# Shift and scale of the first norm: w_mod as the moving operand in four column groups, and identity products in PE's gaps before the first scores

## The chip, the cores and the metric

The kernel runs on one core of a Trainium2 chip. The metric is the device time of one execution in microseconds. The core has five engines with queues of their own: PE (matrix products), DVE (vector), ACT (activation functions), POOL (a second, slower vector engine) and SP (which here only issues DMAs). Engines wait for each other by semaphores; within an engine everything runs in program order.

## The reference

One transformer block on 2048 tokens of width 1024, modulated by a single vector `c`. 32 query heads of width 32 share one key and one value head.

```python
mod = (_silu(c) @ w_mod).reshape(c.shape[0], 6, 1, -1)
sa, ca, ga, sb, cb, gb = ...                 # six vectors of 1024
h = _layernorm(x) * (1 + ca) + sa            # the first norm's scale and shift
x = x + ga * A(h, wq, wk, wv, wo)            # attention: softmax over 2048 keys
h = _layernorm(x) * (1 + cb) + sb
x = x + gb * B(h, w1, w3, w2)                # silu(h w1) * (h w3), times w2; inner width 3584
```

Scale and shift of the first norm are not applied to `x`. The scale `1 + ca` is multiplied into the rows of `wk`, `wv` and `wq`, and the shift `sa` becomes a bias on k, q and v (`sa` times the unscaled weights). So nothing of k or q can be finished before both are known.

## The kernel before

**The graph and its planner.** `build` does not emit instructions in order. It calls `op`, which records a node: engine, a function that gives its instructions, an expected duration, what it reads and writes, a due value `vt`, and a mode for PE (`F` full array, `S` scores in four row groups, `A` four column groups of 32). `Placer.run` then places one node after another on the engine where it can start first by expected durations, and among nodes that can start at nearly the same time takes the one with the lowest `vt` plus an offset. The offsets and four or five parameters come from `PLAN`, one entry for every eight scores, each changing the one before. The program thus holds five fixed queues, with waits where a node needs another engine's result. Some nodes have alternatives (ACT or DVE for a norm or a copy out of PSUM). Almost every instruction is issued by the helper `play` (line 22), so in the profile nearly all carry that line, and tile names tell them apart.

**Banks.** PSUM has eight banks. Six hold scores, in three pairs that are used in turn. Two (6 and 7, `PB` in the profile) serve everything else in sessions (`Sess`): a session keeps its bank until all that reads it is done, and the next session's first product waits for that. The transposes of the first tiles use score banks instead, as no score is due yet.

**The start.** SP issues the tiles of `x` (two tiles per DMA), four 1 MB pieces of `w_mod` (two fields, each in two halves), and `wq` in two pieces. For each of the 16 tiles of 128 tokens, `lnt1` does two halves of statistics (DVE, `ST`), an aggregate (`MV`), three small POOL steps (`RS`, `NB`), the normalization into `XN` (`XNB` or `WO` in the profile, on ACT or DVE), eight transposes on PE against `IDENT`, and a copy into `HT` (ACT or DVE).

`mod_cols(fld)` computes a vector of 1024 as eight columns of 128: for each of eight chunks `c` of the inner width and eight column sets `k`, a product with the weights as stationary operand and one column of silu(c) as moving operand, 64 products in two nodes of 32. DVE then reads eight columns: `MODC[:, 1]` (1 + ca) for field 1, `SAB` (sa) for field 0. `scale0` scales the k and v weights (`WKS`, spread to `WKR`) and the first 256 columns of `wq` (`WQ0S`, in eight pieces on DVE or POOL). `k_bias` and `q_bias` give `KBI` and `QBI`, `k_proj` and `q_proj` fill `KT` and `QT`. All of these go through the two banks.

**The rest.** 512 score steps follow, in the order of `CYC`: the first 16 alternate between two column blocks of heads, since only those q columns are scaled early. A score step is eight products, followed on ACT by two exps into a ring `U` of ten steps. Around them the planner places what else PE has: q projections, value products (`U,V`), row sums (`PS,ONES`), the output projection, and for each of eight blocks of 256 tokens the second norm and the feed-forward part in 14 slabs and four quarters. DVE adds pairs of exps (`PS`), and frees the ring with them. `prods` gives some products two forms, `full` and `cols` (four 32-column products), chosen by the mode PE is in.

## Time and profile before

| | us |
|---|---|
| median of 3 runs | 1138.04 (1136.25 to 1138.82) |
| the profiled execution | 1137.71 |
| its span in the trace | 1135.9 |
| first score on PE | 32.69 |
| first exp on ACT | 33.74 |
| end of the last exp | 1036.25 |
| PE, ACT, DVE, POOL busy | 1108.3, 1021.3, 992.1, 41.3 |

Times in the trace count from the start of the span. In a row of the timeline, the first number is the start, the second the length, then engine, line, instruction, what is written from what, shape and count; a bracket gives idle time ahead of it and what ended that. In a table of stretches, each engine's busy time is followed by the number of its instructions. The rows that the argument uses stand in the prediction.

### The profile page before, as it was taken

What the parts mean: (1) busy time and instruction counts of PE and PEld (TensorE: products, weight loads), DVE (VectorE), ACT (ScalarE), POOL (GpSimd) and SP (SyncE); (2) the same over time, 40 slices, a digit from 0 to 9 for tenths busy, and PEclk for the clock granted to TensorE, in tenths of its full rate; (3) what the DMA queues carried; (4) which work ended last, traced back from release to release, by engine and by line L of the source; (5) the groups of instructions that cost most, each with busy time, mean ns of one, the idle gap of its engine ahead of it and who ended that gap; (6) DMA issues with size and microseconds to landing.
All of it is one profiled execution on the core that took longest, in us unless ns stands there. A gap on an engine that the chain in (4) does not pass through costs nothing.

```text
span 1135.9 us, 38650 instructions
## 1 busy us (share of the span) xinstructions
PE 1108.3 (98%) x17512; PEld 757.2 (67%) x17512; DVE 992.1 (87%) x1614; ACT 1021.3 (90%) x1158; POOL 41.3 (4%) x92
## 2 busy tenths in 40 slices
PE   6899999999999999999999999999999999999998
PEld 6644446666567766777567766777577756776887
DVE  7988999998999889998998899988998889987532
ACT  5999999999999999999999999999999999994110
POOL 5200000000000000000000000000000000000000
PEclk9999999999999999999999999999999999999999
DMA  9320397665486658865596577768597568777993
GB/s 345 106 76 5 128 263 191 175 193 140 114 258 195 174 131 216 235 193 152 128 283 194 149 198 190 219 195 222 130 274 202 150 159 218 207 201 197 246 242 92
DMA packets 381540, 209.72 MB, mean 185 GB/s; under 512 B 17600, under 2 KB 373184, under 8 KB 381376
## 3 DMA queue, kind: packets, MB, share of 16 engines
q1 hardware_dynamic: 380944, 207.11, 65.8%
q8 instruction: 138, 2.26, 0.8%
q14 instruction: 26, 0.21, 0.1%
q10 hardware_dynamic: 432, 0.13, 0.0%
HBM read 199.89 MB, written 4.19 MB: 180 GB/s over the span
## 4 chain that ended last, share of the span: by engine, by line
PE 61%; ACT 25%; DVE 11%; issue 1%; POOL 1%; DMA 0%; DVEq 0%
PE PB L22 44%; ACT U L22 24%; PE S L22 16%; DVE PS L22 4%; DVE ST L22 2%; ACT HT L22 1%; DVE QT L22 1%; POOL RS L22 1%; DVE X L22 1%; DVE HT L22 1%; DVE RB L22 1%; DVE XNB L22 0%; DMA X<-in_A_x_dram 0%; DVE MV L22 0%; DVE RC L22 0%
## 5 line engine op out<-in xcount | busy, mean ns | idle before, releaser
L22 ACT ACTIVATE U<-S 128x1024 bf16<-128x1024 f32 x1024 | 964.6, 1131 | 7.2 <-PE S L22 6.3
L22 DVE TENSOR_TENSOR PS<-U 128x2048 bf16<-128x2048 bf16 x256 | 307.3, 1217 | 9.4 <-ACT U L22 7.9
L22 DVE TENSOR_TENSOR PS<-PS 128x1024 bf16<-128x1024 bf16 (+1 forms) x420 | 282.5, 690 | 3.4
L22 PE MATMUL PB<-QT,W 128*128 128x256 bf16 (+1 forms) x2992 | 229.8, 273 | 1.2 <-DVE HT L22 1.0
L22 PE MATMUL S<-QT,KT 32*128 32x256 bf16 x4096 | 203.8, 273 | 8.0 <-ACT U L22 5.0
L22 PEld LDWEIGHTS PB<-QT,W 128*128 128x128 bf16 (+1 forms) x2992 | 172.3, 97 | 44.3 <-issue 26.5
L22 PE MATMUL PB<-W2S,HT 128*128 128x256 bf16 x1512 | 188.4, 273 | 0.0
L22 PEld LDWEIGHTS PB<-W2S,HT 128*128 128x128 bf16 x1512 | 137.8, 98 | 39.4 <-issue 21.3
L22 PEld LDWEIGHTS S<-QT,KT 32*128 32x128 bf16 x4096 | 60.7, 92 | 139.8 <-ACT U L22 130.1
L22 PE MATMUL PB<-U,V 128*32 128x256 bf16 x4096 | 127.4, 273 | 0.9 <-ACT U L22 0.5
L22 PE MATMUL PB<-QT,HT 128*32 128x256 bf16 (+1 forms) x1560 | 116.0, 273 | 1.5 <-DVE HT L22 1.1
L22 PEld LDWEIGHTS PB<-U,V 128*32 128x32 bf16 x4096 | 101.6, 96 | 21.2 <-issue 12.7
L22 PE MATMUL PB<-HT,W 128*32 128x512 bf16 (+3 forms) x896 | 101.2, 336 | 0.1
L22 PEld LDWEIGHTS PB<-QT,HT 128*32 128x32 bf16 (+1 forms) x1560 | 85.3, 97 | 23.5 <-issue 14.1
L22 ACT ACTIVATE HT<-PB 128x512 bf16<-128x512 f32 (+1 forms) x105 | 74.4, 708 | 12.3 <-PE PB L22 12.3
L22 DVE SCALAR_TENSOR_TENSOR HT<-HT,PB 128x512 bf16<-128x512 bf16 x101 | 69.0, 684 | 8.1 <-ACT HT L22 8.0
L22 PEld LDWEIGHTS PB<-HT,W 128*32 128x32 bf16 (+1 forms) x896 | 51.1, 98 | 33.4 <-issue 10.5
L22 DVE TENSOR_TENSOR HT<-HT,PB 128x512 bf16<-128x512 bf16 x99 | 67.4, 681 | 2.5 <-PE PB L22 1.6
L22 ACT ACTIVATE HT<-S 128x512 bf16<-128x512 f32 (+1 forms) x16 | 11.5, 730 | 54.6 <-PE S L22 54.6
L22 DVE STREAM_TRANSPOSE RB<-PB 128x256 f32<-128x256 f32 x63 | 28.0, 444 | 37.3 <-PE PB L22 36.8
L22 PE MATMUL PB<-WO,QT 128*128 128x512 bf16 (+1 forms) x248 | 56.0, 381 | 1.1 <-DVE RB L22 1.1
L22 POOL TENSOR_SCALAR RS<-MV 128x1 f32<-128x1 f32 x32 | 11.6, 362 | 1004.5 <-DVE MV L22 1003.4
(107 smaller groups left out, 669.5 us busy)
## 6 DMA issues: line engine op xcount, KB each, us to landing
W<-in_B_w_dram SPq DMA_DIRECT2D x150, 512.0 KB, 4.6
W2S<-in_B_w_dram SPq DMA_DIRECT2D x30, 1792.0 KB, 8.5
HT<-in_B_w_dram SPq DMA_DIRECT2D x74, 512.0 KB, 4.6
W2S<-in_w_mod_dram SPq DMA_DIRECT2D x8, 1024.0 KB, 5.7
X<-in_A_x_dram SPq DMA_DIRECT2D x8, 512.0 KB, 7.5
U<-in_w_mod_dram SPq DMA_DIRECT2D x4, 1024.0 KB, 12.1
out_dram<-X SPq DMA_DIRECT2D x7, 512.0 KB, 7.4
W2S<-in_A_x_dram SPq DMA_DIRECT2D x5, 512.0 KB, 9.4
```

The lines of the kernel that those rows point to most:

```text
L22: return getattr(e, call[0])(*call[1], **call[2])
```

## The change

- `mod_cols` turns the operands round. silu(c) of a chunk is spread over 32 columns (`SCR`, a new copy on DVE) and becomes the stationary operand; the weights become the moving operand, 256 columns at a time, in four column groups of the array at once (`tile_position=(0, 32 * g)`). A half is 16 products of 256 columns instead of 32 of one column. The result lies along the free axis, the same in 32 rows of each group, so DVE transposes it in 32 x 32 blocks into `MT` and takes every first column. The nodes are now of mode `A`.
- `keep_warm`, called before a node of mode `F` is placed on PE and before the first score: if the planner expects a gap of at least 0.2 us, it issues products of `IDENT` with itself into score bank 5, as many as the gap holds at 0.075 us each. 70 of them come out.
- The transposes of tile 5 no longer use bank 5 but one of the two shared banks.
- The planner's expected durations of the first transposes and projections are lower.
- `PLAN` is new up to about step 300. The order of all queues follows from it: on PE it differs up to there and is the same from score 288 on; on SP it is the same through the start. All eight pieces of `WQ0S` are on DVE now (five on DVE and three on POOL before); ACT has one KT copy and DVE one HT copy more in the first part.

```diff
-        static = tt < 6
+        static = tt < 5
...
-        op("pe", tr, 0.95 if tt < 4 else 0.6, reads=[("XN", slot), "IDENT"], writes=bk, ...)
+        op("pe", tr, 0.58, reads=[("XN", slot), "IDENT"], writes=bk, ...)
...
+    SCR = Uf[:, 8 * 2048:8 * 2048 + 256].rearrange("p (c r) -> p c r", r=32)
+    MT = Uf[:, 8 * 2048 + 256:8 * 2048 + 1280].bitcast(F32).rearrange("p (x k i) -> p x k i", x=2, i=32)
+    op("dve", lambda: [lambda e: e.tensor_copy(SCR[:], SCC[:, 3, :].unsqueeze(2).broadcast_to([P, NC, 32]))], 0.2, ...)
...
             op("pe", lambda b, h=h: [lambda e, c=c, k=k: e.matmul(
-                BANK[b][:, k:k + 1], WM0[:, c, fld * D:(fld + 1) * D].rearrange("p (q k) -> p k q", k=NC)[:, k, :],
-                SCC[:, 3, c:c + 1], start=(c == 0 and k == 0), stop=(c == NC - 1), skip_group_check=True)
-                for c in range(4 * h, 4 * h + 4) for k in range(NC)], 1.6, ..., mode="F", ...)
+                BANK[b][32 * g:32 * (g + 1), 0:256], SCR[:, c, :],
+                WM0[:, c, fld * D + 256 * g:fld * D + 256 * (g + 1)], start=(c == 0), stop=(c == NC - 1),
+                tile_position=(0, 32 * g), skip_group_check=True)
+                for c in range(4 * h, 4 * h + 4) for g in range(4)], 0.45, ..., mode="A", ...)
+        op("dve", lambda b: [lambda e: e.transpose(MT[:, fld], BANK[b][:, 0:256].rearrange("p (i k) -> p k i", k=NC))], ...)
         if fld:
-            ... e.tensor_scalar(MODC[:, 1, :], BANK[b][:, 0:NC], 1.0, None, ALU.add)
+            ... e.tensor_scalar(MODC[:, 1, :], MT[:, fld, :, 0], 1.0, None, ALU.add)
         else:
-            ... e.tensor_copy(SAB[:], BANK[b][:, 0:NC])
+            ... e.tensor_copy(SAB[:], MT[:, fld, :, 0])
...
+        if e == "pe" and self.warm and self.step == 0 and n.mode == "F":
+            self.keep_warm(start)
...
+    def keep_warm(self, start):
+        product, need = self.warm
+        gap = start - max(self.t["pe"], need.fin)
+        if not need.done or gap < 0.2:
+            return
+        ...
+        sem, count = self.sem, int((gap - 0.05) / 0.075)
+        ...
+            for _ in range(count):
+                play(eng, product(REC))
...
+    pl.warm = (lambda e: e.matmul(BANK[5][:, 0:P], IDENT[:], IDENT[:], start=True, stop=True), ident)
```

The entries of `PLAN` itself are left out.

More of the change, by code (lines that the diff above doesn't have):

```diff
@@ L802, in tr @@
                 IDENT[:]) for cc in range(NC)]
-        op("pe", tr, 0.95 if tt < 4 else 0.6, reads=[("XN", slot), "IDENT"], writes=bk, vt=vt, mode="F", sess=s, post=0.145)
+        op("pe", tr, 0.58, reads=[("XN", slot), "IDENT"], writes=bk, vt=vt, mode="F", sess=s, post=0.145)
         dst = HT[:, :, tt * P:(tt + 1) * P]
@@ L882, in k_proj @@
             BANK[b][:, 0:256], WKR[:, 1, cc].rearrange("p r f -> p (r f)"), HT[:, cc, ts], start=(cc == 0),
-            stop=(cc == NC - 1)) for cc in range(NC)], 1.7 if j == 0 else 0.9, reads=["WKR1"] + hk,
+            stop=(cc == NC - 1)) for cc in range(NC)], 0.9, reads=["WKR1"] + hk,
            writes=[("k", j)], vt=vt, mode="F", sess=s, post=0.145)
@@ L1267, in build @@
     k_proj(0, -1690)
-    q_proj(0, 1, 0, -1690, 2.0)
-    q_proj(0, 1, 1, -1689, 1.5)
+    q_proj(0, 1, 0, -1690)
+    q_proj(0, 1, 1, -1689)
     k_proj(1, -1680)
@@ L1305, in build @@
     G.alias([("U", s, i) for s in range(8) for i in range(2)], [("WM0", fl, h) for fl in range(2) for h in range(2)])
+    G.alias([("U", 8, i) for i in range(2)], ["SCR", ("MT", 0), ("MT", 1)])
     ht = [("HT", cc, tt) for cc in range(NC) for tt in range(NTT)]
```

360 lines of the change are left out of this document (172 added, 188 removed).

## The prediction

> **What bounds the kernel now.** I read the page first, then busy time by stretch, then the start instruction by instruction.
>
> ```profile
> PE 1108.3 (98%) x17512; PEld 757.2 (67%) x17512; DVE 992.1 (87%) x1614; ACT 1021.3 (90%) x1158; POOL 41.3 (4%) x92
> ```
>
> PE is busy 98%, which suggests that less PE work is less time. The stretches say where that holds. I cut them at the starts of scores 0, 10, 16, 32, 64, 128 and 288 of 512, and behind the last exp (columns: stretch, length, then busy us and instructions of PE, PEld, DVE, ACT, POOL; clock, DMA share, GB/s).
>
> ```profile
> 32.69:54.49 21.80, 19.95 (x379) 15.07 (x378) 21.08 (x44) 21.68 (x25) 5.24 (x13) 1.00 0.20 66
> 54.49:65.51 11.02, 10.71 (x188) 4.68 (x189) 10.62 (x13) 11.02 (x13) 0.00 (x0) 1.00 0.01 1
> 65.51:95.75 30.24, 30.22 (x414) 13.28 (x415) 25.98 (x41) 29.86 (x33) 0.00 (x0) 1.00 0.20 72
> 95.75:154.26 58.51, 57.75 (x1129) 28.88 (x1129) 53.42 (x91) 58.51 (x65) 0.00 (x0) 1.00 0.33 110
> 154.26:279.85 125.59, 119.49 (x1861) 77.93 (x1862) 117.20 (x190) 124.57 (x143) 1.60 (x4) 0.99 0.69 188
> 279.85:593.81 313.96, 310.99 (x5077) 209.94 (x5078) 290.38 (x466) 311.60 (x354) 7.33 (x12) 1.00 0.70 189
> 593.81:1036.30 442.49, 440.62 (x7302) 304.43 (x7302) 406.40 (x640) 438.56 (x500) 7.57 (x12) 1.00 0.71 192
> ```
>
> From the first score to 279.85 ACT idles about 1.5 us in all: the exps set the pace there, and PE's 98% is mostly company. Only in scores 16 to 32 is PE full (30.22 of 30.24) while ACT waits. From 279.85 on both are nearly full. So time can be won in three ways: exps that start earlier, less other work on ACT behind that start, and shorter ACT waits. The start itself, on PE and then on DVE:
>
> ```profile
> 20.69 1.06 PE L22 MATMUL PB<-IDENT,XNB 128*128 128x128 bf16 x8
> 21.55 2.06 PE L22 MATMUL PB<-SCC,U 128*128 128x1 bf16 x32
> ...
> 24.96 2.88 PE L22 MATMUL PB<-HT,WO 128*128 128x256 bf16 x16 [0.25 <-DVE KBI L22]
> ...
> 28.41 2.79 PE L22 MATMUL PB<-HT,WO 128*128 128x256 bf16 x24 [0.19 <-ACT KT L22]
> 32.07 0.69 PE L22 MATMUL PB<-IDENT,WO 128*128 128x128 bf16 x8 [0.86 <-DVE MV L22]
> 32.69 0.40 PE L22 MATMUL S<-QT,KT 32*128 32x256 bf16 x8
> ```
> ```profile
> 22.68 0.71 DVE L22 TENSOR_SCALAR WO<-W,MODC 128x256 bf16<-128x256 bf16 x2 [0.20 <-DMA W<-in_A_wq_dram]
> 23.65 0.17 DVE L22 CAST SAB<-PB 128x8 bf16<-128x8 f32 x1 [0.27 <-PE PB L22]
> ...
> 24.75 0.16 DVE L22 COPY KBI<-PB 128x1 f32<-128x1 f32 x1 [0.21 <-PE PB L22]
> ...
> 26.26 2.42 DVE L22 BATCH_NORM_STATS2 ST<-W2S 128x6 f32<-128x512 bf16 x4
> ...
> 31.45 0.47 DVE L22 TENSOR_SCALAR QT<-PB,QBI 128x256 bf16<-128x256 f32 x1
> ...
> 55.93 0.42 DVE L22 COPY WO<-PB 128x256 f32<-128x256 f32 x1 [0.28 <-PE PB L22]
> ```
>
> The transposes tell the array's speed: eight take 1.06 us at 20.69 and 0.69 at 32.07, so the array is slow until the k products. The first score waits for QT. QT waits for the DVE queue and the q products, those for two alternating banks, and the scaled q weights for `wq`, on which DVE waited at 22.68.
>
> **The change, part by part.**
>
> *The four `mod_cols` blocks.* 128 one-column products (2.06 us per 32) become 64 of 256 columns, four abreast. The trace has that form elsewhere:
>
> ```profile
> 54.82 1.29 PE L22 MATMUL PB<-U,V 128*32 128x256 bf16 x40
> ```
>
> 1.29/40 is 32 ns each, so a block of 16 takes 0.5 us, 1.0 at half speed. That takes 4 to 6 us off PE, all ahead of score 0. DVE gets for each field a transpose of 128x256 (nearest row: one half-sum copy of that size at 55.93, 0.42 us; its input is strided, so up to twice that) and a copy like SAB's (0.17). The last block starts when its weights land instead of behind transposes at 21.55: I put SAB at about 21.5, where it ended at 23.82. But SP's order is the same through the whole start, so `wq` lands at 22.7 as before, and of these 2.3 us only 0 to 1 reach what follows.
>
> *The scaling of the first q weights.* The program's order puts all eight pieces on DVE; before, POOL did three.
>
> ```profile
> L22 DVE TENSOR_SCALAR W<-W,MODC 128x1024 bf16<-128x1024 bf16 x8 | 3.8, 481 | 0.1
> L22 DVE COPY HT<-PB 128x1024 bf16<-128x1024 bf16 x5 | 3.3, 680 | 0.0
> ...
> L22 DVE TENSOR_SCALAR WO<-W,MODC 128x256 bf16<-128x256 bf16 x5 | 1.5, 351 | 0.2 <-DMA W<-in_A_wq_dram 0.2
> ```
>
> One piece costs between 0.12 (a quarter of 481 ns) and 0.35; I take 0.25, since what the 351 holds of POOL's company goes: 2.0 us, to 24.7. Next on DVE come one statistics half (0.61) and the KBI copy, done at 25.45. The k products wait for it, because it frees their bank. The Trainium skill, "SBUF — State Buffer", section "SBUF: two separate sides", says that VectorE in a two-port mode and GpSimd shut each other out for whole instructions. By that rule a piece is near 0.12 and KBI comes 1.0 us sooner; the 351 beside POOL agrees, but no row shows a piece alone.
>
> *From KBI to the first score.* k0 runs 25.5 to 26.4 (28.41 row: 24 in 2.79, eight in 0.93); ACT empties it (0.47) by 27.05. QBI stands behind two more halves on DVE, so k1 runs 26.9 to 27.8, q0 to 28.7, q1 to 29.6. DVE does four halves (2.42) behind QBI and empties q0 by 29.9. First score: 30.0 instead of 32.69. If k0 and k1 run as in the 24.96 row (eight in 1.44), q1 ends at 30.2 and the score comes at 30.3; with all four at half the fast speed, at 31.2.
>
> *The identity products.* There are 70, in gaps the planner foresees. At the slow transposes' 0.13 us they are 9 us, 46 of them ahead of the 1+ca block. They read IDENT and write a bank that transposes now leave alone; PE's own queue alone waits for them. If a gap is shorter than foreseen, the transposes behind come up to 1 us late, and the wait for `wq` covers that.
>
> *What the exps win.*
>
> ```profile
> 33.74 1.01 ACT L22 ACTIVATE U<-S 128x1024 bf16<-128x1024 f32 x1
> 34.64 1.02 ACT L22 ACTIVATE HT<-PB 128x1024 bf16<-128x1024 bf16 x1
> 35.78 1.24 ACT L22 ACTIVATE XNB<-W2S,NB,RS 128x1024 bf16<-128x1024 bf16 x1
> ...
> 87.11 91.87 ACT L22 ACTIVATE U<-S 128x1024 bf16<-128x1024 f32 x100 [0.35 <-PE S L22]
> ```
> ```profile
> 29.50 0.47 ACT L22 ACTIVATE KT<-PB,KBI 128x256 bf16<-128x256 f32 x1 [1.14 <-PE PB L22]
> ```
>
> A score at 30.0 puts the first exp at 30.6, 3.1 us earlier (an HT copy stood ahead of it before). But ACT's new order has two KT, two norms and two HT copies behind the first exp, about 4.9 us at the distances between these rows, where it had two HT copies and a norm, 3.0. That leaves 1.2. DVE limits it further. From 22.68 to the first half-sum copy at 55.93 it hardly rests (1.4 us). It now starts at the same landing with one HT copy, one norm (as a W piece, 0.48) and three q pieces more, one KT and the SAB cast less: 0.6 to 1.5 us more. The half sums free the exps' buffers and PE's banks. So term A, the lead at score 16, lies between -0.5 and 1.6. I take **0.7**.
>
> *Scores 16 to 32.* 32 exps at 0.919 us (91.87/100) are 29.4; the stretch took 30.24 because PE was full. In the new order it holds 1.3 us less PE work (32 U,V products at 32 ns, and a net two 512-column products). Term B: **0.8**, between 0 and 0.85.
>
> *Scores 64 to 288.* ACT idles 1.0 + 2.4 us in 154.26 to 593.81, the most this part can give. Counting the order, by score 160 about 5 us more PE work is done than before, by 288 exactly as much, and from there PE's order is the same to the end, so a lead at 288 is kept. PE gets lighter where it was level with ACT (scores 176 to 208 and 240 to 272, by 0.5 to 1.7 us per 16 scores) and heavier at 80 to 160 (0.8 to 2.2), where PE had 6.1 us idle in 154.26 to 279.85. Term C: **0.9**, between -1 and 2.0.
>
> The sum is 0.7 + 0.8 + 0.9 = 2.4. The profiled execution took 1137.71 (span 1135.9 and 1.8 around it), 0.3 below the median 1138.04 and within the runs. 1137.71 - 2.4 = **1135.3**.
>
> **The rivals.**
>
> *1. The clock falls back before the k products.* PE can slow itself by waiting: after the wait in the first row the second stretch was granted half the clock.
>
> ```profile
> 176.28 0.40 PE L22 MATMUL S<-QT,KT 32*128 32x256 bf16 x8 [1.44 <-ACT U L22]
> ```
> ```profile
> 178.00:180.00 2.00, 2.00 (x17) 0.91 (x15) 1.93 (x3) 1.52 (x3) 0.00 (x0) 0.50 0.08 25
> ```
>
> In the new start PE waits some 2 us for KBI, with only one-column products and a few identity products around. Half speed for k and q puts the score at 31.2, so term A at about -0.5: 1136.5. Against it: the wait is short and the array was fed just before. The Trainium skill, "TensorE: Matmul & The Clock Gate", section "Part 1: The HAM clock gate (the "warmup" mystery)", gives about 3.4 us of sustained activity to full speed and an idle window of that length back to half. By it this goes either way, as the window runs free; the 178 row agrees.
>
> *2. DVE holds the start.* Its queue from 22.68 is at least as long as before. If the half sums come no earlier than 55.93, A is 0 and, with PE's gaps only moved, C is 0 too: 1137.71 - 0.8 = 1136.9. For it: 21.08 of 21.80. Against it: ACT, not DVE, was never idle there.
>
> *3. Slower: PE becomes the bound at scores 80 to 176.* There the new order raises PE's sum to within 0.5 to 1.1 us of ACT's per 16 scores (31.8 against 32.3 at 96 to 112). The sum counts 0.11 us for a full product of 256 columns (28.41 row: 2.79/24), a quarter for one four abreast, and 0.1 for a change of array mode (32.69 row: 0.40 for eight four abreast, whose columns are 0.26). It decides from about 3% more than the sum; at 6% the six stretches lose about 7 us, of which PE's lighter work behind them gives back 2.4: 1142. Against it: in scores 16 to 32 such a sum gave 30.0 and the trace 30.24.
>
> *4. The blocks do not stream abreast.* Then a block takes 16 x 0.18 = 2.9 us (24.96 row) instead of 2.06, SAB comes near 24 and the score 1.5 later: A at -0.8, 1136.8. The 32 ns of the U,V row speak against it.
>
> **How the numbers follow.** 0.2% of 1138.04 is 2.3 us, about what a measurement of this kernel can tell from no change; faster by over that means under 1135.8. Forecast 0.56, rival 1 0.10, rival 2 0.17, rival 3 0.14, rival 4 0.03. Of the forecast's own range (A, B, C at their ends together give 1133.3 to 1138.2; ends rarely meet, so mostly 1133.3 to 1136.8) about 0.46 lies under 1135.8; a little of rivals 1 and 2 does too: faster 0.50. Rival 3 and the worst of the rest give slower 0.14; same 0.36. The range reaches from the forecast's low end past rivals 1, 2 and 4 to 1138.6 and leaves out rival 3.
>
> **What would show it.** Right: first score near 30.0, with `wq` still landing at 22.7; eight WQ0S pieces in about 2 us; score 16 some 0.7 and score 32 some 1.5 earlier; ACT's idle time from score 64 to 288 under 3.4 us; everything behind score 288 shifted by one amount. Wrong: k products of 1.4 us and more for eight (rival 1), half-sum copies at 56 with ACT waiting ahead of score 11 (rival 2), ACT waits for S at scores 80 to 176 (rival 3), blocks over 2 us (rival 4).

## The result and the profile after

The changed kernel takes 1143.27 us (median of five runs, 1141.81 to 1145.23) against 1137.81 (five runs, 1136.25 to 1138.82). The ratio is 1.0054, 95% interval [1.0038, 1.0071]: 5.5 us slower (4 to 8 by the interval), where 1135.3 had been forecast. The profiled execution is the one of 1143.27 us; its span is 1141.5.

The line of busy times on the page, and from PE's list of waits the line that the kernel before does not have (columns: total us, times, longest):

```profile
PE 1104.5 (97%) x17732; PEld 753.8 (66%) x17758; DVE 992.0 (87%) x1620; ACT 1020.9 (89%) x1158; POOL 41.4 (4%) x89
```
```profile
PE PB L22 <- issue: 5.8, 14, 1.9
```

Every engine works as long as before, within 4 us; what grew is idle time (PE's from 27.6 to 37.0 us). "issue" means that PE waited for nothing that the profile shows. Of its 14 times, three are waits, of 1.92, 1.73 and 0.36 us; the other eleven, of 0.16 us each, lie where the trace lacks the record of a product (it has 26 products less than weight loads). The stretches, cut at the same scores as before (0, 10, 16, 32, 64, 128, 288, end of the exps):

```profile
30.21:54.88 24.67, 21.45 (x385) 16.69 (x387) 22.62 (x51) 22.70 (x26) 8.14 (x21) 0.93 0.29 95
54.88:67.69 12.81, 12.49 (x181) 6.31 (x184) 12.59 (x15) 11.91 (x13) 0.00 (x0) 1.00 0.01 1
67.69:97.07 29.38, 28.64 (x450) 12.38 (x451) 25.91 (x40) 29.03 (x33) 0.00 (x0) 1.00 0.21 74
97.07:155.46 58.39, 56.93 (x1178) 29.13 (x1183) 53.41 (x96) 58.39 (x65) 0.00 (x0) 1.00 0.34 110
155.46:280.43 124.97, 119.64 (x2000) 79.64 (x2003) 117.66 (x188) 124.62 (x143) 2.44 (x4) 1.00 0.71 195
280.43:599.10 318.67, 311.19 (x5119) 207.61 (x5124) 288.42 (x463) 311.58 (x354) 9.19 (x12) 0.99 0.68 184
599.10:1042.00 442.90, 439.70 (x7273) 304.29 (x7279) 406.32 (x640) 438.73 (x500) 8.42 (x12) 1.00 0.71 192
```

Against the same stretches of before, the first is 2.87 us longer (24.67 against 21.80), the second 1.79 longer, the third 0.86 shorter, the fourth and fifth together 0.74 shorter, the sixth 4.71 longer. The first score comes 2.47 us earlier, as forecast. Everything is lost behind it, in two places: scores 0 to 16, and somewhere in scores 128 to 288.

**The start on PE:**

```profile
21.53 0.62 PE L22 MATMUL PB<-U 128*32 128x256 bf16 x16 [1.26 <-DMA U<-in_w_mod_dram]
...
26.12 1.05 PE L22 MATMUL PB<-HT,WO 128*128 128x256 bf16 x8 [0.75 <-DVE KBI L22]
27.38 2.79 PE L22 MATMUL PB<-HT,WO 128*128 128x256 bf16 x24 [0.21 <-DVE QBI L22]
30.21 0.40 PE L22 MATMUL S<-QT,KT 32*128 32x256 bf16 x8
...
35.43 0.40 PE L22 MATMUL S<-QT,KT 32*128 32x256 bf16 x8 [0.82 <-ACT U L22]
...
37.26 0.58 PE L22 MATMUL S<-QT,KT 32*128 32x256 bf16 x8 [0.78 <-ACT U L22]
37.77 1.89 PE L22 MATMUL PB<-HT,WO 128*128 128x256 bf16 x8
39.45 1.70 PE L22 MATMUL PB<-IDENT,XNB 128*128 128x128 bf16 x16
...
42.95 0.40 PE L22 MATMUL S<-QT,KT 32*128 32x256 bf16 x8
```

and the clock there, in stretches of 1 us:

```profile
36.00:37.00 1.00, 0.48 (x8) 0.34 (x6) 1.00 (x3) 1.00 (x2) 0.83 (x2) 1.00 0.88 281
37.00:38.00 1.00, 0.74 (x10) 0.29 (x11) 1.00 (x6) 1.00 (x2) 0.00 (x0) 0.67 1.07 378
38.00:39.00 1.00, 1.00 (x6) 0.71 (x5) 0.62 (x2) 1.00 (x2) 0.81 (x3) 0.50 1.01 341
```

The k products run at full speed at 26.12 (eight in 1.05). Then PE waits 0.82 us ahead of score 2 and 0.78 ahead of score 3, both times for ACT, and from 37.3 the granted clock is at half, for 3.41 us: eight k products take 1.89 us, 16 transposes 1.70. ACT stands idle for 1.30 us behind them, since the order has an HT copy next, which needs those transposes:

```profile
30.66 1.02 ACT L22 ACTIVATE U<-S 128x1024 bf16<-128x1024 f32 x1 [1.73 <-PE S L22]
...
40.54 1.02 ACT L22 ACTIVATE HT<-PB 128x1024 bf16<-128x1024 bf16 x1 [1.30 <-PE PB L22]
```

**Scores 147 and 213.** Rows of PE's timeline at both places, and the stretches around the first:

```profile
317.30 1.27 PE L22 MATMUL PB<-QT,W 128*32 128x256 bf16 x39
320.50 2.09 PE L22 MATMUL PB<-QT,W 128*32 128x256 bf16 x9 [1.92 <-issue]
```
```profile
452.89 1.05 PE L22 MATMUL PB<-QT,HT 128*128 128x256 bf16 x8 [1.73 <-issue]
```
```profile
318.00:320.00 2.00, 0.57 (x23) 0.29 (x12) 1.97 (x4) 2.00 (x3) 0.00 (x0) 1.00 1.16 292
320.00:322.00 2.00, 1.50 (x8) 0.94 (x8) 0.21 (x1) 0.18 (x1) 0.00 (x0) 0.66 1.16 294
322.00:324.00 2.00, 2.00 (x16) 0.94 (x15) 1.38 (x2) 0.82 (x1) 0.00 (x0) 0.50 0.61 219
```

PE stops ahead of the last of 40 four-column products: 39 are in the first row, the 40th begins the second, and the eight behind it are of the full form. The DMA engines are full (share 1.16; the recorded times of the transfers overlap, so that they add up to more than the time of 16 engines). Half clock follows the first wait, from 320.65 to 324.06; behind the second the clock held. Between scores 144 and 148 the lead falls from -1.85 to -5.61, between 208 and 216 from -5.40 to -7.45.

The trace also holds PE's instruction packets, 16 KB each. The page counts 140 of them in this queue (packets, MB, share):

```profile
q8 instruction: 140, 2.29, 0.8%
```

With 17,732 products, 17,758 weight loads and 274 instructions of PE's sequencer, that is one packet for some 255 instructions. Counted between their starts, 126 of the 140 distances are 150 to 350 instructions. The packets of 317.88 and 450.27 started after 472 and 481. So the theory: the packet comes late because the DMA engines are full, PE uses up what it has, and the four-column form (48 instructions and 48 weight loads for what 12 and 12 do in the full form) uses it up four times as fast.

### The profile page after: what moved, and what is told of

It reads as the page before. It is cut to its first block, busy times and chain, and to the rows that moved or that the text cites. A ratio compares the mean times of both kernels' runs of the same rounds, so it can differ in the third digit from the quotient of the medians.

```text
span 1141.5 us, 39122 instructions
## 1 busy us (share of the span) xinstructions
PE 1104.5 (97%) x17732; PEld 753.8 (66%) x17758; DVE 992.0 (87%) x1620; ACT 1020.9 (89%) x1158; POOL 41.4 (4%) x89
## 4 chain that ended last, share of the span: by engine, by line
PE 62%; ACT 19%; DVE 13%; POOL 2%; issue 1%; DMA 1%; SPq 1%
PE PB L22 46%; ACT U L22 18%; PE S L22 17%; DVE PS L22 6%; POOL RS L22 2%; DVE ST L22 2%; DVE X L22 1%; DMA W<-in_A_wq_dram 1%; DVE QT L22 1%; ACT HT L22 1%; DVE RB L22 1%; DVE HT L22 1%; SPq L22 1%; DVE XNB L22 0%; DVE WO L22 0%
## 5 line engine op out<-in xcount | busy, mean ns | idle before, releaser
L22 PE MATMUL PB<-QT,W 128*32 128x256 bf16 (+1 forms) x3288 | 230.4, 274 | 2.6 <-issue 1.9
L22 PEld LDWEIGHTS PB<-QT,W 128*32 128x32 bf16 (+1 forms) x3288 | 172.5, 97 | 45.1 <-issue 27.5
L22 PE MATMUL PB<-QT,HT 128*128 128x256 bf16 (+1 forms) x1288 | 118.2, 273 | 2.6 <-issue 1.7
L22 PEld LDWEIGHTS PB<-QT,HT 128*128 128x128 bf16 (+1 forms) x1288 | 85.7, 97 | 26.5 <-issue 15.5
L22 PE MATMUL PB<-HT,W 128*32 128x512 bf16 (+3 forms) x1075 | 98.2, 327 | 3.9 <-issue 1.3
L22 PE MATMUL PB<-WO,QT 128*128 128x512 bf16 (+1 forms) x260 | 52.9, 380 | 2.2 <-DVE RB L22 0.8
L22 POOL TENSOR_SCALAR RS<-MV 128x1 f32<-128x1 f32 x32 | 14.2, 444 | 1010.6 <-DVE MV L22 1009.0
```

The costliest lines, as they stand in the source:

```text
L22: return getattr(e, call[0])(*call[1], **call[2])
```

## The experiments

Leads in us (start of a score in the profile of before, minus the same in this kernel; minus is later), and times with ratios to the runs of before on the same chip:

| kernel | time | ratio, 95% interval | s0 | s4 | s10 | s16 | s32 | s64 | s148 | s216 | s288 | s511 |
|---|---|---|---|---|---|---|---|---|---|---|---|---|
| after | 1143.27 | 1.0054 [1.0038, 1.0071] | +2.47 | +0.54 | -0.39 | -2.18 | -1.33 | -1.19 | -5.61 | -7.45 | -5.29 | -5.66 |
| e1_full_two | 1139.95 | 1.0021 [1.0011, 1.0030] | +2.67 | +1.14 | +0.18 | -1.60 | -0.75 | -0.62 | -1.53 | -1.24 | +0.75 | +0.42 |
| e2_no_products | 1146.26 | 1.0071 [1.0056, 1.0086] | +1.41 | +0.94 | +0.01 | -1.78 | -0.93 | -0.79 | -6.43 | -7.54 | -5.55 | -5.89 |
| e3_kb_fill | 1142.5 | 1.0045 [1.0028, 1.0063] | +2.55 | +1.99 | +1.03 | -0.75 | +0.09 | -2.49 | -7.62 | -9.43 | -7.28 | -7.61 |
| e4_light_w | 1139.04 (one run) | | +2.57 | +0.97 | +0.03 | -1.76 | -0.91 | -0.77 | -1.83 | -3.03 | -0.87 | -1.45 |
| e8_old_mod | 1149.18 | 1.0093 [1.0071, 1.0114] | -0.39 | -2.23 | -3.19 | -4.97 | -4.12 | -3.99 | -10.60 | -11.64 | -9.65 | -9.97 |
| e9_front94 | 1139.94 | 1.0022 [1.0012, 1.0032] | +1.42 | -0.72 | -1.61 | -3.40 | -2.55 | -3.91 | -4.82 | -5.92 | -3.93 | -4.25 |
| e10_front60 | 1142.02 | 1.0040 [1.0026, 1.0055] | +2.20 | +1.63 | +0.69 | -1.10 | -0.25 | -1.53 | -3.42 | -3.69 | -1.70 | -2.03 |
| e11_kb_front80 | 1139.06 | 1.0012 [1.0004, 1.0021] | +0.81 | +0.36 | -0.59 | -2.38 | -1.53 | -1.39 | -2.32 | -2.87 | -0.89 | -1.23 |
| e6_kb_full | 1138.59 | 1.0007 [0.9998, 1.0016] | +2.62 | +2.05 | +1.10 | -0.69 | +0.16 | -1.18 | -2.58 | -2.74 | -0.74 | -2.14 |
| e7_full_all | 1138.35 | 1.0006 [0.9998, 1.0014] | +3.00 | +2.43 | +1.48 | -0.31 | +0.36 | -1.01 | -2.14 | -2.08 | -0.10 | -1.26 |
| e13_mc_fill | 1137.34 | 0.9988 [0.9979, 0.9997] | +2.64 | +2.07 | +1.13 | -0.66 | +0.19 | -0.19 | -1.83 | -1.56 | +0.42 | +0.06 |
| e5_before_cols | 1137.64 | 1.0000 [0.9992, 1.0009] | -0.18 | -0.18 | -0.18 | -0.18 | -0.18 | -0.19 | +1.19 | +0.97 | +1.10 | +1.18 |
| e12_before_cols_front | 1140.87 | 1.0032 [1.0018, 1.0045] | -1.22 | -1.24 | -1.24 | -1.24 | -1.24 | -1.25 | +0.12 | -2.95 | -3.29 | -3.22 |

The leads are those of one profiled execution each; the times are medians. Runs of one kernel spread over 1 to 5 us, so a lead at the end and a median can differ by over 2 us (e1_full_two, e10_front60: the profiled run was their fastest).

### The form: e1_full_two

```diff
             if n.col is not None:
+                if n.col[1][0] is None:
+                    self.forced[id(n.col[1])] = 136 <= self.step <= 152 or 200 <= self.step <= 218
                 n.col[1][0] = self.mode
-                fn = n.col[0] if self.mode == "C" else fn
+                fn = n.col[0] if self.mode == "C" and not self.forced[id(n.col[1])] else fn
```

> The changed kernel with the same order, but products whose bank session opens at scores 136 to 152 or 200 to 218 are issued in their full form (one product of 128 columns) instead of four of 32 columns. Theory: the changed kernel's two long waits on PE with no releaser (1.92 us at 318.6, 1.73 us at 451.2) are PE running out of instructions: 472 and 481 instructions lie between two instruction packets there, where it is usually about 256. The full form has a quarter of the instructions, so both waits go, the slow clock behind them too, and the lead lost at scores 144 to 152 (3.4 us) and 208 to 216 (2.1 us) comes back: 1143.3 - 5 = about 1138. Rival: the waits belong to the place (busy DMA queues, a buffer), not to the form; then they stay and the time stays at 1143, or rises by some tenths for the extra changes of array mode.

The long waits are gone and 3.3 us of the 5.5 come back; the time stays 2 us above the expected 1138, though the profiled run, with 1137.16, comes near it. Where PE stood still, the timeline now has

```profile
316.37 2.14 PE L22 MATMUL PB<-QT,W 128*128 128x256 bf16 x18
```

The same work, a quarter of the instructions, no pause. From score 32 to 288 this kernel gains 1.50 us on before.

### The transfers: e4_light_w

```diff
+            cs = slice(0, 1) if n == 1 else slice(0, NC)
-            dma("sp", W13SL[r][:, m], w[:, ...].rearrange("(c p) f -> p c f", p=P), ...)
+            dma("sp", W13SL[r][:, m, cs], w[:, ...].rearrange("(c p) f -> p c f", p=P)[:, cs], ...)
```

and the same for `w2`: most bytes of the second token block's feed-forward weights are left out, order and number of DMAs stay.

> The changed kernel with the same order, leaving out most of the weight loads of the second block of 256 tokens (one of eight rows of each w1 and w3 slab, one of 28 of each w2 quarter is loaded; the same number of DMAs). Theory: PE's instruction packets come late when the DMA engines are full of weight traffic. With the traffic of the second block gone the packet near 317.9 comes about 256 instructions behind the one before it, the wait at 318.6 goes, and the wait at 451, in the third block's traffic, stays. Rival: the packets are late whatever the traffic, since 32-column products use instructions four times as fast; then both waits stay.

The stretches 312 to 320 of the kernel after, and of this one:

```profile
312.00:316.00 4.00, 3.95 (x111) 2.79 (x113) 4.00 (x6) 4.00 (x6) 0.00 (x0) 1.00 1.16 314
316.00:320.00 4.00, 2.57 (x87) 1.85 (x76) 3.93 (x7) 3.85 (x5) 0.00 (x0) 1.00 1.16 316
```
```profile
312.00:316.00 4.00, 4.00 (x132) 3.12 (x136) 3.96 (x6) 4.00 (x6) 0.00 (x0) 1.00 0.07 20
316.00:320.00 4.00, 4.00 (x85) 2.77 (x76) 3.96 (x8) 3.85 (x5) 0.00 (x0) 1.00 0.43 112
```

With a DMA share of 0.07 and 0.43 instead of 1.16, PE runs through the same four-column products without a pause. The second wait, in the next block's traffic, which was left as it is, stays (1.63 us).

### The identity products at the start: e2_no_products

```diff
-            for _ in range(count):
-                play(eng, product(REC))
```

> The changed kernel with the same order, without the 70 identity products. Theory: they bring the array to full speed early, but the start waits for wq and the DVE queue; without them the k products run slow (1.4 us for eight instead of 1.05) and the first score comes 0.3 to 1.0 us later than 30.21. The end moves by less than 1 us. Rival: they are what keeps the start fast; then the first score comes at 31.5 or later and the time rises by over 1 us. Since PE has 140 instructions fewer, the places where its instruction packets fall shift as well, and the two long waits at scores 144 to 152 and 208 to 216 may move or go, which would bring up to 5 us by itself.

The first score is 1.07 us later than in the kernel after, so the products do what they are for. The lead at score 4 is nevertheless 0.40 larger than with them, and at 16 too. That compares two clocks: in the kernel after the clock fell at score 3, in this run it held from 29.4 to 319.5 us. Against e3_kb_fill below, whose clock held there as well, the products are worth 1.14 us at the first score, 1.05 at score 4 and 1.03 at score 16, so what they bring is carried on. And the time is 3 us worse, for a reason that has nothing to do with the start: 70 products and their weight loads are 140 PE instructions less, so every packet falls due 140 places later in the program. One wait grew (2.85 us at 315.97, 500 instructions between packets), the other shrank to 0.20, and two shorter ones are new (0.40 and 0.75 us, at 341 and 388 us).

### The clock at score 3: e3_kb_fill

```diff
-            stop=(cc == NC - 1)) for f in range(f0, f1) for cc in range(NC)], ...
+            stop=(cc == NC - 1)) for f in range(f0, f1 - 1) for cc in range(NC)] + [lambda e: e.matmul(
+            BANK[b][:, 2 * P:3 * P], IDENT[:], IDENT[:], start=True, stop=True)] * (14 if f0 else 0) + [
...
```

> The changed kernel with the same order, and 14 identity products put into the node of the second q bias, in unused columns of its bank, between scores 1 and 2, where PE waits 0.82 us for ACT. Theory: the lead of 3.5 us at score 2 is lost by score 4 because PE, after two waits of 0.8 us, falls to half clock at 37.4, and the k product and two tiles' transposes there take 1.3 us longer than at full clock, which ACT waits out; with the gap filled the clock stays, score 4 comes 1.0 to 1.5 us earlier than 42.95, and the time falls by about 1 us. Rival: the order is at fault (four tiles' transposes ahead of score 4, two copies ahead of its exps): score 4 stays within 0.4 us of 42.95.

The 14 products fill PE's wait ahead of score 2. One wait of 0.80 us is left, ahead of score 3, and the clock holds:

```profile
37.51 1.05 PE L22 MATMUL PB<-HT,WO 128*128 128x256 bf16 x8
38.40 1.45 PE L22 MATMUL PB<-IDENT,XNB 128*128 128x128 bf16 x16
...
41.50 0.40 PE L22 MATMUL S<-QT,KT 32*128 32x256 bf16 x8
```

Score 4 comes 1.45 us earlier than in the kernel after and score 32 1.42: the start's clock costs 1.4 us and nothing behind swallows that. It does not show in the time, because 28 more instructions move the packets again: a new wait of 1.12 us at 143.75, with 475 instructions between packets, and the half clock from 147.7 to 151.2 us took more than that (lead +0.09 at score 32, -2.49 at 64).

What is left of the loss shows in scores 10 to 16 of this kernel:

```profile
53.46:66.27 12.81, 12.81 (x183) 6.32 (x185) 12.58 (x15) 11.91 (x13) 0.00 (x0) 1.00 0.01 1
```

PE is full there, 12.81 of 12.81, where before did with 10.71 of 11.02. The new order does the value products and projections earlier, and the exps wait for that; scores 16 to 32 are 0.84 us faster for it. ACT's row shows the wait ahead of the first exp of score 10; one of 0.35 us ahead of score 16 follows it, also for PE. Before, ACT had none there.

```profile
55.22 11.15 ACT L22 ACTIVATE U<-S 128x1024 bf16<-128x1024 f32 x12 [0.90 <-PE PB L22]
```

### Streaming itself: e8_old_mod

```diff
-                BANK[b][32 * g:32 * (g + 1), 0:256], SCR[:, c, :],
-                WM0[:, c, fld * D + 256 * g:fld * D + 256 * (g + 1)], start=(c == 0), stop=(c == NC - 1),
-                tile_position=(0, 32 * g), skip_group_check=True)
-                for c in range(4 * h, 4 * h + 4) for g in range(4)], ...
+                BANK[b][:, g:g + 1], WM0[:, c, fld * D:(fld + 1) * D].rearrange("p (q k) -> p k q", k=NC)[:, g, :],
+                SCC[:, 3, c:c + 1], start=(c == 0 and g == 0), stop=(c == NC - 1), skip_group_check=True)
+                for c in range(4 * h, 4 * h + 4) for g in range(NC)], ...
```

> The kernel after with the shift and scale computed as before: 32 products of one column to a half, and a copy instead of the block transposes; order, identity products and everything else as in the kernel after. If streaming the weights is what brings the first score forward, the blocks take 1.5 to 2.1 us each again instead of 0.6, SAB comes 1 to 2 us later and the first score at 31.0 to 32.0 instead of 30.2. By the theory that the start's lead is lost by score 16 whatever the first score is (ACT's and DVE's queues and PE's work in scores 10 to 16 set it), score 16 moves by under 0.5 us, and the time is that of the kernel after within 1.5 us: 1142 to 1145. If the first score's time is carried through, everything is 1 to 2 us later than the kernel after: 1144.5 to 1146.

```profile
23.47 2.03 PE L22 MATMUL PB<-SCC,U 128*128 128x1 bf16 x32
...
33.08 0.40 PE L22 MATMUL S<-QT,KT 32*128 32x256 bf16 x8
...
322.87 0.38 PE L22 MATMUL PB<-QT,W 128*32 128x256 bf16 x4 [3.08 <-issue]
```

The blocks are computed as before, and a copy stands in for the block transpose. The last block ends at 25.5 instead of 22.15 and the first score is 2.87 us later. The expectation that score 16 would not move was wrong: it is 2.79 later. So the streamed products are worth 2.8 us in this order, and they arrive in full (the clock fell at score 3 in both kernels). The time lies above both expected ranges. Scores 144 to 148 lose 5.56 us instead of 3.76, in the longer wait at 319.8; another 1.5 us comes behind the last score and was not followed up.

### Only the place of the packets: e9_front94, e10_front60

If the packets are the cause, work that does nothing must help when it moves them to another place. Both kernels only add one-column products, in the first 9 us, where PE waits for `w_mod`: 94 in e9, 60 in e10. They read `IDENT` and write one column of bank 5.

```diff
+        def _run(eng):
+            eng.wait_ge(sem[need.sem], need.val)
+            for _ in range(94):
+                play(eng, product(REC))
```

> The kernel after with 94 more products on PE, of one column of the identity, issued at the very start, where PE waits 9 us for the first weights. They only add work, but move every later PE instruction 188 places on against the packets of 256 instructions. In the kernel after and its variants a packet falls due when about 225 of the instructions fetched are left and comes 3 to 5 us later while the DMA engines are full; PE waits where it uses up what is left in that time. Counted in the trace, a packet that falls due at scores 144 to 146 or 209 to 211 is late in that sense. With 188 places more none falls due there (they come at scores 141 and 147, 208 and 212). The packet theory: no PE gap without a releaser of over 0.7 us near scores 147 and 213, lead at the end of -2 to 0 instead of -5.7, 1138.5 to 1140.5. The rival, that the form itself or another wait behind it costs the time: gaps as in the kernel after, 1142.5 to 1144. A warm array at the start may bring the first score up to 0.3 us forward in either case.

> The same with 60 instead of 94 products at the start (120 places). By the same count packets then fall due at scores 145 and 210, in the thick of the four-column products and of the transfers. The packet theory: both gaps are there again, 1.5 to 3 us each, lead at the end -5 to -8, 1142 to 1146. If it is the products at the start that help or hurt (a warmer array, a later start), 60 act like 94: within 1 us of that run.

94 products take the kernel from 1143.27 to 1139.94, although its first score comes 1.06 us later than in the kernel after; 60 leave it at 1142.02. The remaining waits, of the first kernel and of the second:

```profile
448.29 1.05 PE L22 MATMUL PB<-QT,HT 128*32 128x256 bf16 x30 [1.29 <-issue]
```
```profile
317.37 0.51 PE L22 MATMUL PB<-QT,W 128*32 128x256 bf16 x12 [0.77 <-issue]
...
447.15 0.29 PE L22 MATMUL S<-QT,KT 32*128 32x256 bf16 x4 [0.46 <-issue]
```

With 94, the wait at score 147 is gone as expected, though 465 instructions lay between two packets there: it was in time by little. The one at 213 is 1.29 instead of 0, a miss. With 60, both are there as expected but shorter than the 1.5 to 3 us; this profile is of the fastest of four runs (1140.11 to 1143.73). Where a packet falls due decides that PE is in danger. How late it comes then seems to vary from run to run; with one profile for each kernel this is not shown.

### A wait made in the kernel before: e5_before_cols, e12_before_cols_front

```diff
+                if n.col[1][0] is None:
+                    self.forced[id(n.col[1])] = 144 <= self.step <= 150
-                fn = n.col[0] if self.mode == "C" else fn
+                fn = n.col[0] if self.mode == "C" or self.forced[id(n.col[1])] else fn
```

> The kernel before, with the sessions on PE that open at scores 144 to 150 issued in the four-column form; nothing else differs. If the long waits of the kernel after come from how fast PE uses up its instructions while the DMA engines are full, the same wait appears here, where the kernel before had none: one gap of 0.7 to 2.2 us on PE without a releaser at 316 to 325 us, where more than about 450 PE instructions lie between two instruction packets, half clock for some 3 us behind it, scores behind 160 later by 1.5 to 4 us, and a time of 1139 to 1141.5. If the waits come from the order that the kernel after has (a buffer or a transfer that is late only there), the form changes nothing: no such gap, scores behind 160 within 0.5 us of the kernel before, 1137.0 to 1138.2.

No wait of over 0.20 us came, and the time is that of before: the first theory, form and traffic, was not enough. (The lead of 1.2 us from score 80 on has another cause: in this run the clock held behind the wait at score 75, where it fell in the profile of before.) The packets lay at 312.72 and 318.19, with 343 and 306 instructions. The second kernel adds 56 one-column products at the start, which by themselves only make everything 1.2 us later:

> The kernel before, with the sessions of scores 144 to 150 in the four-column form as in the earlier run, and 56 one-column products at the start of PE (112 places). In that earlier run a packet fell due at score 147 and was there 2.8 us later, in time. With 112 places more one falls due at score 146 (about 313.6 us), with 263 PE instructions in the 4 us behind it, more than the 225 that are left. The packet theory: a PE gap of 0.5 to 2.5 us at 316 to 319 us and half clock behind it, 1139 to 1141.5. If form and place cannot stop PE in this order (or the packet comes within 3 us again), the time stays at 1137 to 1138.2.

```profile
321.12 1.49 PE L22 MATMUL PB<-QT,W 128*32 128x256 bf16 x47 [1.32 <-issue]
```
```profile
333.10 1.26 PE L22 MATMUL PB<-QT,W 128*32 128x256 bf16 x37 [1.63 <-issue]
```

The wait is there, with 470 instructions to the packet of 318.59. A second wait, from 331.47, had not been foreseen; only 343 instructions lie ahead of its packet, but the one before had come late. The lead falls from +0.12 at score 148 to -2.95 at 160. Form, full DMA engines and the place of the packet together make the wait at score 147; in these runs any one of them taken away removes it.

A count over all the traces leaves little room for another cause. Eleven of these kernels have waits on PE of 0.2 us or more without a releaser, 26 in all. Take PE's recorded instructions (products, weight loads, those of its sequencer) up to such a wait, and 256 for every packet that had started before the one that ends it. In 23 of the 26 the first number is the second plus 449, to the instruction; in the three of the kernel after it is so to within one when the 15 to 18 products without a record are added. PE goes on 2.3 to 2.8 us after the packet's start in 24 of them, 3.3 in two. A buffer or a transfer that is late would not keep to a step of 256 instructions.

### All mends together: e6_kb_full, e7_full_all, e11_kb_front80, e13_mc_fill

e6 joins the 14 products of e3 and the full form of e1 (also for scores 50 to 62), e7 takes the full form everywhere, e11 has the 14 products and 80 one-column products in front.

> The kernel after with both mends together: 14 identity products in the second q-bias node, which fill PE's wait ahead of score 3, and the full form for sessions that open at scores 50 to 62, 136 to 152 and 200 to 218. If clock and packets are separate causes, the gains add: scores 4 to 32 as in the run with the identity products (lead +2.0 at score 4, -0.75 at 16, about 0 at 32), no PE gap near 143, 319 and 452 us, a lead of 1 to 2 us at score 288 and at the end, and 1136 to 1138 (the run with the full form had 1139.95, less 1.4). If the time won at the start is swallowed later by PE's or ACT's load in scores 64 to 288, the lead at 288 stays at the 0.75 of the run with the full form alone, and the time at 1139 to 1140.5.

> As the run before it on the list (14 identity products), but every product that has two forms is in the full form throughout, so PE uses the fewest instructions. By the packet theory no PE gap of over 0.7 us without a releaser is left anywhere and no two packets lie more than about 400 instructions apart; a product costs the same stream time in both forms (0.11 us for a full one, four times 0.03), so only array mode changes are added, some 0.1 us each at scores where the mode would have been kept: 1136 to 1139. If the form in itself is what costs (mode changes outweigh the packets), it comes out at 1140 to 1143 with PE full in scores 64 to 288.

> The 14 identity products in the second q-bias node and 80 one-column products at the start: 188 places again, in the other causes' favour too. If the clock's loss at scores 3 and 4 and the late packets are all that went wrong, the lead is +2.0 at score 4, -0.7 at 16, about 0 at 32, and 0 to +1 at the end: 1136.5 to 1138. If PE's heavier load at scores 80 to 210 costs more than it gives back behind 240, the end is at -1 to -2: 1138.5 to 1139.5.

All three come near before and none beats it. The gains at the start add as expected (+2.0 to +2.4 at score 4 in e6 and e7); in e11 the products in front cost 1.7 us at the first score, so its lead at score 4 is 0.36 and not 2.0. e7 shows that the form as such costs nothing that can be measured here; two of its packets still lie 449 and 434 instructions apart, where under 400 was expected, and no wait came of it. The profiled run of e6, its slowest, has two short late packets (0.48 us at 383, 0.81 at 1020; the second takes the lead from -1.06 at score 500 to -2.14). But e6 and e7 lose 1.4 us between scores 48 and 64 without any late packet. The clock fell there, behind two blocks of one-column products (`SCC,W2S`, 64 in all); here e6:

```profile
146.00:148.00 2.00, 1.90 (x24) 0.51 (x21) 2.00 (x8) 2.00 (x3) 0.00 (x0) 0.74 0.90 304
148.00:150.00 2.00, 2.00 (x6) 0.52 (x4) 1.11 (x1) 1.33 (x2) 0.00 (x0) 0.50 0.67 229
```

The last kernel, e6 with two products of the identity behind every eight of these 64:

```diff
-            stop=(cc == NC - 1)) for k in range(4) for cc in range(NC)], 0.85, ...
+            stop=(cc == NC - 1)) if cc < NC else e.matmul(
+            BANK[b][:, 2 * P:3 * P], IDENT[:], IDENT[:], start=True, stop=True)
+            for k in range(4) for cc in range(NC + (2 if i in (5, 6) else 0))], 0.85, ...
```

> The kernel with both mends (14 identity products in the second q-bias node; the full form for sessions of scores 50 to 62, 136 to 152 and 200 to 218), and 16 more products of the identity with itself among the 64 one-column products at scores 58 and 59, two behind every eight. If the one-column products are what lets the clock fall, it stays at 1.00 from 144 to 152 us, the lead at score 64 is 0 to +0.4 (the products cost up to 0.4 us) instead of -1.2, and the time 1137.0 to 1138.2 instead of 1138.6. If the clock falls for another reason (a short wait, the transfers), 0.50 appears there again in the profile, the lead at 64 is about -1.5 and the time 1138.5 to 1139.

```profile
146.00:148.00 2.00, 1.95 (x44) 1.13 (x42) 1.70 (x6) 1.82 (x3) 0.00 (x0) 1.00 0.60 191
148.00:150.00 2.00, 1.99 (x22) 0.63 (x20) 2.00 (x4) 1.88 (x3) 0.00 (x0) 1.00 0.96 335
```

The clock holds, and the time is 1137.34 against 1138.43, 0.9988 [0.9979, 0.9997]: the one version that beats before, by 0.3 to 2.4 us. Score 64 comes 1.0 us earlier than in e6. The 32 instructions that were added move the packets as well, and the two late ones of e6 are not in this profile, so the clock need not be all of the gain. Its eleven runs lie within 0.9 us, the fifteen of before within 4.5. Much of the gain is that the bad runs are gone: its fastest run, 1136.90, is slower than the fastest of before, 1136.66. This was one kernel on one chip; other places of the same products were not tried.

## Why the prediction was wrong

Two steps of the sum failed. Term C priced PE's products by their stream time alone and the number of PE's instructions at nothing: late instruction packets took 5.5 us. Term A counted the queues of ACT and DVE and left out PE: its own work in scores 10 to 16 took 1.45 us, and the clock that fell behind its new waits 1.4.

| term | forecast | after | without its accident |
|---|---|---|---|
| A, lead at score 16 | +0.7 | -2.18 | -0.75 (e3_kb_fill) |
| B, scores 16 to 32 | +0.8 | +0.85 | +0.84 (e3_kb_fill) |
| C, scores 32 to 288 | +0.9 | -3.96 | +1.50 (e1_full_two) |
| behind 288 | 0 | -0.37 | -0.33 (e1_full_two) |

**The first score** came at 30.21 (forecast 30.0) and the first exp at 30.66 (30.6). The blocks took 0.62 us (0.5 to 1.0), and rival 4 falls with that. The shift was ready late, at 22.8 instead of 21.5: the last quarter of `w_mod` landed only at 21.5, which the step on the blocks took for the end of the whole. As the text said that only 0 to 1 of it reaches what follows, it cost little. On DVE:

```profile
22.20 0.45 DVE L22 STREAM_TRANSPOSE U<-PB 128x256 f32<-128x256 f32 x1 [0.88 <-PE PB L22]
22.68 0.17 DVE L22 CAST SAB<-U 128x8 bf16<-128x8 f32 x1
23.27 2.13 DVE L22 TENSOR_SCALAR WO<-W,MODC 128x256 bf16<-128x256 bf16 x8 [0.42 <-DMA W<-in_A_wq_dram]
...
39.69 0.48 DVE L22 TENSOR_SCALAR KT<-PB,KBI 128x256 bf16<-128x256 f32 x1 [1.07 <-PE PB L22]
```

The transpose is at the low end of its bounds (0.45). The eight pieces took 2.13 (2.0 forecast), after `wq` landed 0.6 later than before. They also bear on the question of the shared port:

```profile
23.27 0.96 DVE L22 TENSOR_SCALAR WO<-W,MODC 128x256 bf16<-128x256 bf16 x2 [0.42 <-DMA W<-in_A_wq_dram]
```
```profile
22.92 1.04 POOL L22 COPY WO<-SAB 128x1024 bf16<-128x1024 bf16 x1 [3.49 <-DVE SAB L22]
```

The first piece took 0.76 us while POOL's copy ran, until 23.96; the other seven followed every 0.2 us. The Trainium skill, "SBUF — State Buffer", section "SBUF: two separate sides", says that the two engines shut each other out for whole instructions. This row of the trace agrees. The kernel before does not show it so plainly: there two of DVE's pieces, of 0.42 and 0.27 us, began and ended inside one of POOL's of 1.04 (POOL's spans are rough). The 0.12 that was worked out for a piece alone is too little; without POOL beside it a piece took 0.27.

**Rival 1** was looked for in the wrong place. For the first k products the clock held (1.05 us for eight). It fell 11 us later, behind two waits for ACT that no step had costed: score 2 and score 3 come earlier, but the exps and the ACT work between them do not, so PE waits for free buffers. This is term A's first error, 1.4 us by e3. The mechanism stood in the prediction, with the row of 176.28; what failed was to ask where else the new order makes PE wait. Its price, 1.2 us on term A, was near the 1.4 that this fall cost. That it fell there is in part chance: e2 and e10 have both waits (0.59 and 0.78, 0.82 and 0.79), and there the clock held.

**Term A's second error** is the count of work. Term B was right, +0.85, since 1.3 us of PE work leave scores 16 to 32. But that work went into scores 10 to 16, which have only twelve exps to hide it: PE's busy time there is 12.49 us instead of 10.71, and the stretch grew by 1.79; 1.25 of it are ACT's two waits for PE (0.90 and 0.35, in e3 as in the kernel after). The step for term A counted ACT's and DVE's queues and left PE's out, though the prediction had found PE full in the stretch right behind. A and B are one sum, about 0.1 in e3, not 0.7 + 0.8.

**Rival 2**, DVE holds the start, was half right: the half sums came at 57.8 instead of 55.93. In the kernel after they were late because DVE's KT copy waited 1.07 us for the slow k products (the last row above); with the clock mended they come at 56.40, still not earlier than before, but PE is the one that is full and that ends ACT's waits.

**Term C.** Without late packets 1.50 us are won (e1; bounds -1 and 2.0), but not by the mechanism of the forecast, shorter waits of ACT in the new order. 0.87 of it lies between scores 72 and 80, where the profile of before held a fall of the clock of its own. From score 64 to 288 before took 439.55 us; e5, whose order is that of before, took 438.26 with the clock held there, and e1 took 438.18. ACT's idle time in these scores is 3.38, 2.49 and 2.53 us. Where both have that fall, e13 took 438.93 against 439.55. So the order itself brings 0.1 to 0.6 us, and that e1's 1.50 lies within the bounds is luck. **Rival 3**, PE's load at scores 80 to 176, came about in small: e1 takes 1.2 us longer there than before, ACT waiting 0.81 instead of 0.23, and gets 1.9 back in scores 240 to 272.

What the sum did not hold was any price for the number of instructions. The counts of before and after stood side by side and products of four columns were priced by their stream time, 32 ns, alone. The lead falls by 5.8 us at the two late packets (3.76 at scores 144 to 148 and 2.05 at 208 to 216), of which e1 loses 1.1 without them. Over scores 32 to 288 the packets cost 5.5 us (-3.96 against +1.50), as much as the whole result.

**Behind score 288** the shift is one amount within 0.4 us, as forecast.

So of the 8 us between forecast and result (in leads +2.4 and -5.66), 5.5 are late packets, 1.4 is the clock at score 3, 1.45 is the rest of term A (0.7 forecast, -0.75 in e3), PE's work in scores 10 to 16, and 0.4 lies behind score 288; term C brought 0.6 more than forecast beside the packets, by the clock of before.

Two sums of the prediction do not come out. The low ends of A, B and C (-0.5, 0 and -1) give 1139.2 and not 1138.2; the result lies outside that too. Rival 3's 1142 is 1137.7 + 7 - 2.4, without terms A and B; with them it is 1140.8.

## What to carry to other kernels

Leaving an engine waiting early is not free even when the wait itself is: list the new waits of PE that a better start makes, and fill them or expect the clock to fall. When work is moved out of a full stretch, price it again in the stretch where it lands. And count PE's instructions as well as their stream time: where transfers fill the DMA engines, a form with four times the instructions can stop PE, and a change anywhere ahead moves the places where this happens, so a difference of 3 us between two nearly equal kernels may come from nothing else; some do-nothing products in an idle stretch tell it.

## What the runs showed of the hardware

**PE's instructions come by the same DMA engines as the data.** There is one 16 KB packet per 255 instructions. PE has fetched 449 instructions and 256 for every packet before, by the count at the waits. While the DMA engines are nearly idle (share under 0.2), a packet starts when 180 to 313 of the fetched ones are left, mostly 212 to 275. With a DMA share of 1.0 to 1.2 it starts up to 4.5 us later than that, and PE stops for up to 3.1 us where it uses up the rest meanwhile. Ahead of the waits of over 1 us lay 434 to 500 instructions between two packets (343 once, in e12), though 465 (e9) and 449 (e7) passed without one. The Trainium skill, "Runtime: NRT & Kernel Launch", section "Instruction fetch mechanics", gives blocks of 16 KiB, 256 instructions, fetched by the sequencer through a DMA queue of its own while it works on the one before, and calls the crossing mostly hidden. The size agrees with these runs. That it is hidden does not hold here: the waits were 1.92 and 1.73 us in the kernel after and 3.08 in e8_old_mod.

**The clock fell without one long pause.** Two waits of 0.82 and 0.78 us within 3 us were enough at 37 us in the kernel after, two of 0.82 and 0.79 were not in e10, and one of 0.80 was not in e3. Two blocks of one-column products, which the profile shows as a busy PE, brought it down in e3, e6, e7, e9 and e10 and not in the kernel after, e1, e2, e4, e8 and e11, which have the same instructions there; with full products among them it held in e13.

The clock records of the 15 traces put this in order. All changes of one execution lie on a grid of 3.413 us, to 2 ns, so the clock is set once in a window of that length. For each window from 25 to 1040 us I added up what PE streamed, a product of 256 columns on the full array as 1, one on a quarter of the array as a quarter, a one-column product as 1/256 (24 full ones take 2.79 us in the 27.38 row). Each of the 20 falls comes behind a window with at most 12.1. Of some 4,400 windows at full clock, only 14 with as little were followed by full clock. So it is the work in a window that counts, not one pause, and the same waits weigh differently as the window's border falls.

The Trainium skill, "TensorE: Matmul & The Clock Gate", section "Part 1: The HAM clock gate (the "warmup" mystery)", speaks of an idle window of about 3.4 us that runs free of the kernel. The length and the free run agree with the grid; an idle window does not fit the fall at 37.34 us, where PE was busy for 1.80 of the 3.41 us ahead of it.
